# Decode attention with a gated dense branch: part of one weight load split into sixteen transfers of a few rows

## The chip, the cores and the metric

One core of a Trainium2 chip. The metric is the device time of one execution in microseconds (us).

## What is computed

A decode step for two sequences of one token each (B = 2), model width 448, everything in float32:

```
g = sigmoid((x * gate_w).sum(-1))
q = (x @ wq)                       # 16 heads of 256
p = softmax(q . k_cache / 16)      # 4096 cached positions per head
a = concat(p . v_cache) @ wo
b = relu(x @ w1 + b1)**2 @ w2 + b2
out = g * a + (1 - g) * b
```

The caches hold 2 x 16 x 4096 x 256 numbers each, 134 MB; with the weights some 290 MB pass through the core, each byte once.

## The kernel before

The work of attention is cut into 16 rounds: 8 pairs of heads times 2 sequences. A round takes 8.4 MB of keys and 8.4 MB of values. 128 partitions hold them, 64 for each head of the pair, and each partition has 64 positions in one contiguous row of 64 KB. Keys go into two buffers in turn (`keys[0]`, `keys[1]`; both are named `k` in the profile), values into one (`vals`, named `v`). In a round VectorE multiplies the keys by the query in place (L218) and sums over the 256 (L235), TensorE brings the maxima together, ScalarE takes the exponential (L255), and TensorE multiplies the probabilities by the values (`values`, in a loop of 15 rounds on the chip, and once more for the last). The output of each head pair is normed, turned and kept in `oT`.

The buffers carry weights as well. Before the rounds `keys[1]` holds `wq` (7.3 MB), and the lower part of `vals`, up to `spare` = 12,544 numbers of each partition, holds `wf`, that is `w1` and `w2` laid out by rows (6.4 MB; 50,176 B of each partition). After the last round's values have been used, `vals` takes `wo` in five pieces.

All large loads go through one queue, that of SyncE (SP), by the helper `load` (its issue is L116). The order is: `wq` (L170), the keys of round 0 (L171), `wf` (L172), the keys of round 1 (L206, held until TensorE has finished with `wq`), the values of round 0 (L232, held until TensorE has finished with `wf` and the dense branch), and from there keys (L248) and values (L243) in turn, each held until its buffer is free. The first three wait for nothing. `pk` (x, gate, b1; L169) and `b2` (L173) are issued by ScalarE (ACT).

Each load raises a semaphore by 16 when it has landed; `load` returns the count so far. For `wf` that is `FL`. TensorE waits for it at one place, ahead of the hidden layer (the matmuls into `fin`), where the code before has `pe.wait_ge(FL.h, 16)`. Behind that wait TensorE computes the hidden layer and turns it (`sm`), VectorE applies bias, relu and square (L228 to L231), and TensorE adds the second dense product into `acc`. All matmuls go through the helper at L289.

At the end TensorE takes the last values (`po`), turns them (`ot`), and multiplies `oT` with `wo`: 24 blocks into `acc`, 8 into `fin`; the first 16 blocks need the first piece of `wo`. Then VectorE copies the result (L276), and SP sends it out (L279).

Of the kernel before, what the change touches and what calls it, by code (L numbers as in the profile page):

```python
# [10 lines left out]
P = 128  # L11
# [2 lines left out]
WO_CUTS = (0, 16, 24, 28, 31, 32)  # L14
V_CUT = 48
HELP = 24


class Count:
# [16 lines left out]
def gated_mix_kernel(nc, b2, wq, wf, wo, k_cache, v_cache, out):  # L36
# [18 lines left out]
    pe, dve, act, pool, sp = nc.tensor, nc.vector, nc.scalar, nc.gpsimd, nc.sync  # L55
# [3 lines left out]
    def sb(name, *free):  # L59
        return nc.alloc_sbuf_tensor(name, [P, *free], F32)[:]  # L60
# [5 lines left out]
    vals = sb("v", PLACE)  # L66
# [30 lines left out]
    QL, FL, BL, SL = (Count(nc, n + "_landed") for n in ("wq", "wf", "b2", "small"))  # L97
# [9 lines left out]
    spare = w2_at + FC * D  # L107
# [3 lines left out]
    def kv(cache, r):  # L111
        t, b = rounds[r]
        return cache[b, 2 * t:2 * t + 2].rearrange("h (p j) d -> (h p) (j d)", j=KEYS)

    def load(dst, src, sem, after=None):
        ins = sp.dma_start(dst, src)  # L116
        if after:
            after[0].on(ins, after[1])
        return sem.up(ins, 16)
# [49 lines left out]
    SL.up(act.dma_start(pk, wq[:, 3 * N + N // 2:3 * N + N // 2 + PK]), 16)  # L169
    load(keys[1][:, :3 * N + N // 2], wq[:, :3 * N + N // 2], QL)  # L170
    load(keys[0], kv(k_cache, 0), KL[0])  # L171
    load(vals[:, :spare], wf, FL)  # L172
    BL.up(act.dma_start(b2r, b2), 16)  # L173


# [31 lines left out]
    for r, (t, b) in enumerate(rounds):  # L207
# [4 lines left out]
        elif r == 4:  # L212
            dve.wait_ge(AC.h, AC_QB[-1])
        help = HELP if r == R - 1 else 0
        s = scores[r == R - 1]

        def times_q(lo, hi):
            return DV.up(KL[r % 2].on(dve.tensor_tensor(kt[:, lo:hi], kt[:, lo:hi], q.unsqueeze(1).to_broadcast([P, hi - lo, DH]), op=ALU.mult), 16 * (r // 2 + 1)))  # L218
# [7 lines left out]
        n = times_q(help, KEYS)  # L226
# [139 lines left out]
            pe.wait_ge(AC.h, AC_QB[i - 4])  # L366
        done(mm(QBANK[i % 4], halves[:, u * B + b, :], qs[:, a, :]), TE_QB[i])

    pe.wait_ge(FL.h, 16)
    for c in range(CF + 1):  # L370
        for n in range(4):
            if c < CF:
# [36 lines left out]
    for i, (t, k) in enumerate(blocks):  # L409
# [9 lines left out]
        n = i - early  # L419
# [72 lines left out]
```

## Time and profile before

| | us |
|---|---|
| median of 3 runs | 676.64 |
| lowest and highest run | 676.58, 892.45 |
| profiled execution, its own time | 676.61 |
| its span, first to last instruction | 675.3 |
| VectorE busy | 560.0 |
| TensorE busy (matmuls) | 218.2 |
| ScalarE busy | 45.8 |

SP's queue is q1 in the profile, ACT's is q10, and q8 and q14 carry instructions to the engines. A packet is one contiguous piece that one of the core's 16 DMA engines moves. The queue view lists packets, MB and the time of the packets as a share of 16 engines over the window that was asked for; a packet counts in the window where it starts, with its whole time, so in a window of a few hundred ns the share can pass 100%. "Under 512 B" counts the small packets; in SP's queue of this kernel these are, but for the output, the 4-byte writes that raise a semaphore when an engine has done its part of a transfer. In the timeline a row has start, duration, engine, line, operation, tiles, and in brackets how long the engine was idle before and what ended that. "SPq" rows are SP's issues.

### The profile page before, as it was taken

The numbers are of one execution on the slowest core, as the hardware profiler recorded it, in microseconds if no ns is written. First come the engines' busy times: TensorE is split into PE (matmuls) and PEld (weight loads), VectorE is DVE, ScalarE is ACT, GpSimd is POOL, SyncE is SP. The second block draws the span as 40 slices with busy tenths as digits, with TensorE's granted clock in tenths as the row PEclk, the third lists the DMA queues.
The fourth block names the chain that finished last, engine by engine and source line by source line (L and its number), as shares of the span: only waits on it lengthen the run. The fifth ranks groups of instructions, "written<-read, shape, count | busy, mean of one in ns | idle before, by whom it ended". The sixth has DMA issues, their size and how long they took to land. (4 is left out here: it accounts for less than half of the span.)

```text
span 675.3 us, 3522 instructions
## 1 busy us (share of the span) xinstructions
PE 218.2 (32%) x1522; PEld 67.9 (10%) x1522; DVE 560.0 (83%) x120; ACT 45.8 (7%) x159; POOL 2.1 (0%) x15
## 2 busy tenths in 40 slices
PE   0725042140605124060503206060411506050386
PEld 0111001010101101010100101010110101010022
DVE  1067999999979797998979798997979799797920
ACT  0121000000000000000000000000000000001400
POOL 1000000000000000000000000000000000000000
PEclk9977556585756557575655757575665757576577
DMA  9999999999999999999999999999999999999997
GB/s 381 431 453 421 435 435 436 435 435 431 431 435 435 435 435 435 435 435 435 435 435 435 435 435 435 435 431 435 435 427 435 435 435 435 435 435 431 422 415 305
DMA packets 5923, 289.63 MB, mean 429 GB/s; under 512 B 797, under 2 KB 926, under 8 KB 1182
## 3 DMA queue, kind: packets, MB, share of 16 engines
q1 hardware_dynamic: 5772, 289.54, 99.2%
q8 instruction: 3, 0.05, 0.0%
q10 hardware_dynamic: 146, 0.02, 0.0%
q14 instruction: 2, 0.02, 0.0%
HBM read 289.55 MB, written 0.00 MB: 429 GB/s over the span
## 5 line engine op out<-in xcount | busy, mean ns | idle before, releaser
L218 DVE TENSOR_TENSOR k<-k,q 128x16384 f32<-128x16384 f32 (+2 forms) x17 | 275.7, 16220 | 52.4 <-DMA k<-in_k_cache_dram 52.4
L235 DVE TENSOR_REDUCE s<-k 128x64 f32<-128x16384 f32 x15 | 258.2, 17211 | 0.0
L289 PE MATMUL po<-v,p 128*4 128x512 f32 x960 | 139.6, 746 | 294.4 <-PEq L293 294.4
L289 PEld LDWEIGHTS po<-v,p 128*4 128x4 f32 x960 | 26.8, 99 | 394.4 <-issue 394.4
L194 ACT ACTIVATE o<-po 128x512 f32<-128x512 f32 x16 | 9.6, 597 | 438.0 <-PE po L289 438.0
L289 PE MATMUL mt<-ident,m 128*64 128x64 f32 x64 | 7.6, 328 | 82.3 <-PEq L293 82.3
L289 PE MATMUL ot<-rl,o 128*128 128x2 f32 x128 | 16.4, 250 | 15.6 <-PEq L293 15.6
L289 PEld LDWEIGHTS ot<-rl,o 128*128 128x128 f32 x128 | 15.5, 191 | 30.0 <-issue 30.0
L255 ACT ACTIVATE p<-s,nb 64x64 f32<-64x64 f32 x30 | 10.5, 350 | 96.1 <-DVE nb L239 95.9
L289 PE MATMUL sm<-rsm,ones 128*128 128x2 f32 x32 | 8.9, 348 | 21.3 <-PEq L293 21.3
L239 DVE TENSOR_REDUCE nb<-mt 128x1 f32<-128x64 f32 x16 | 3.6, 225 | 13.0 <-PE mt L289 13.0
L176 DVE TENSOR_TENSOR y<-pk 128x8 f32<-128x8 f32 x1 | 0.2, 169 | 16.8 <-DMA pk<-in_wq_dram 16.8
L289 PEld LDWEIGHTS mt<-ident,m 128*64 128x64 f32 x64 | 5.1, 200 | 83.9 <-issue 83.9
L235 DVE TENSOR_REDUCE s_last<-k 128x40 f32<-128x10240 f32 x1 | 10.8, 10810 | 0.0
L289 PEld LDWEIGHTS sm<-rsm,ones 128*128 128x128 f32 x32 | 8.0, 310 | 23.7 <-issue 23.7
L273 DVE COPY wide<-oT 128x2 f32<-128x2 f32 x8 | 0.7, 165 | 11.7 <-ACT oT L195 11.7
L224 ACT ACTIVATE k<-k 128x256 f32<-128x256 f32 x24 | 9.6, 400 | 8.5 <-DVE k L218 8.5
L289 PE MATMUL fin<-v,pk 128*2 128x448 f32 x32 | 4.9, 775 | 16.0 <-DMA v<-in_wf_dram 16.0
L289 PE MATMUL pq<-k,pk 128*2 128x512 f32 x64 | 9.9, 787 | 0.0
L289 PE MATMUL po<-k,p 128*4 128x512 f32 x64 | 9.4, 753 | 0.5 <-DMA k<-in_v_cache_dram 0.5
L276 DVE COPY y<-fin 128x112 f32<-128x112 f32 x1 | 0.3, 275 | 10.2 <-PE fin L289 10.2
L289 PE MATMUL acc<-v,oT 128*2 128x448 f32 x48 | 7.1, 765 | 2.1 <-DMA v<-in_wo_dram 2.1
(64 smaller groups left out, 68.3 us busy)
## 6 DMA issues: line engine op xcount, KB each, us to landing
k<-in_wq_dram SPq DMA_DIRECT2D x1, 7168.0 KB, 19.7
v<-in_wf_dram SPq DMA_DIRECT2D x1, 6272.0 KB, 53.0
k<-in_v_cache_dram SPq DMA_DIRECT2D x1, 6144.0 KB, 37.8
v<-in_wo_dram SPq DMA_DIRECT2D x1, 3584.0 KB, 17.9
k<-in_v_cache_dram SPq DMA_DIRECT2D x1, 2048.0 KB, 42.4
v<-in_wo_dram SPq DMA_DIRECT2D x1, 1792.0 KB, 21.8
v<-in_wo_dram SPq DMA_DIRECT2D x1, 896.0 KB, 23.6
v<-in_wo_dram SPq DMA_DIRECT2D x1, 672.0 KB, 24.7
```

Source lines behind the costliest of these rows:

```text
L176: DV_Y = DV.up(SL.on(dve.tensor_tensor(y, xT[:, :CF + 1, :].rearrange("p c b -> p b c"), pk[:, 10:14].unsqueeze(1).to_broadcast([P, B, CF ...
L194: OC.up(TE.on(act.activation(o, po, AF.Copy), te_val(r)))
L218: return DV.up(KL[r % 2].on(dve.tensor_tensor(kt[:, lo:hi], kt[:, lo:hi], q.unsqueeze(1).to_broadcast([P, hi - lo, DH]), op=ALU.mult), 16 ...
L224: ins = act.activation(kt[:, j], kt[:, j], AF.Copy, accum_out=s[:, j:j + 1])
L235: DV_S = DV.up(DV.on(dve.tensor_reduce(s[:, help:], kt[:, help:], axis=AX.X, op=ALU.add), n))
L239: DV_NB = DV.up(TE.on(dve.tensor_reduce(nb, mt[:, :64], axis=AX.X, op=ALU.max, negate=True), te_mt(r)))
L255: e = act.activation(p8[z, :, hh:hh + 3:2], s[z].rearrange("p (m s) -> p m s", s=2), AF.Exp, bias=nb[z], accum_out=rsm[z, hh:hh + 1])
L273: DV_W = dve.tensor_copy(wide[:, n, 0:W:16], o_block(t, k))
L276: DV_Y4 = DV.up(TE.on(dve.tensor_copy(y4, fin[:, :DQ]), TE_FIN))
L289: return pe.matmul(dst, lt, rhs, start=start, stop=stop)
```

## The change

The first 128 numbers (512 B) of each of the 128 rows of `wf` leave the one transfer, which now takes 49,664 B of each row. They follow it in sixteen transfers on the same queue, of 8, 1, 15, 14, 13 and so on down to 2 rows; the rows are taken in order from partition 0 to 127. All raise the same semaphore, and TensorE waits for the sum of the seventeen.

```diff
+FIRST = 128
+ROWS = [8, 1] + list(range(15, 1, -1))
...
     load(keys[0], kv(k_cache, 0), KL[0])
-    load(vals[:, :spare], wf, FL)
+    load(vals[:, FIRST:spare], wf[:, FIRST:], FL)
+    p0 = 0
+    for n in ROWS:
+        load(vals[p0:p0 + n, :FIRST], wf[p0:p0 + n, :FIRST], FL)
+        p0 += n
+    assert p0 == P
     BL.up(act.dma_start(b2r, b2), 16)
...
-    pe.wait_ge(FL.h, 16)
+    pe.wait_ge(FL.h, FL.n)
     for c in range(CF + 1):
```

SP's instructions from the program's start, before (a size is partitions x numbers; `pe`, `dve` are the semaphores of TensorE and VectorE):

```order
L116 DMA k<-in_wq_dram 128x14336 [waits barrier_Pool_Activation_PE_DVE_SP_release]
L116 DMA k<-in_k_cache_dram 128x16384
L116 DMA v<-in_wf_dram 128x12544
L116 DMA k<-in_k_cache_dram 128x16384 [waits pe]
L116 DMA v<-in_v_cache_dram 128x16384 [waits pe]
```

And with the change, the same place down to the fourth of the small transfers (lines have moved by two):

```order
L118 DMA k<-in_wq_dram 128x14336 [waits barrier_Pool_Activation_PE_DVE_SP_release]
L118 DMA k<-in_k_cache_dram 128x16384
L118 DMA v<-in_wf_dram 128x12416
L118 DMA v<-in_wf_dram 8x128
L118 DMA v<-in_wf_dram 1x128
L118 DMA v<-in_wf_dram 15x128
L118 DMA v<-in_wf_dram 14x128
```

The small ones go on in this way; here their last three, and what follows on SP:

```order
L118 DMA v<-in_wf_dram 4x128
L118 DMA v<-in_wf_dram 3x128
L118 DMA v<-in_wf_dram 2x128
L118 DMA k<-in_k_cache_dram 128x16384 [waits pe]
L118 DMA v<-in_v_cache_dram 128x16384 [waits pe]
```

The sixteen stand between `wf` and the keys of round 1, without a wait of their own; SP has 57 issues where it had 41. On the other engines no instruction moves.

## The prediction

> **What bounds the kernel now.** I read the page's slices first, then the chain that ended last, then VectorE and the SP queue in order of time, and last narrow windows of the DMA view.
>
> ```profile
> DMA  9999999999999999999999999999999999999997
> GB/s 381 431 453 421 435 435 436 435 435 431 431 435 435 435 435 435 435 435 435 435 435 435 435 435 435 435 431 435 435 427 435 435 435 435 435 435 431 422 415 305
> q1 hardware_dynamic: 5772, 289.54, 99.2%
> ```
>
> The 16 DMA engines are busy 99.2% of the span in SP's queue (q1), at 435 GB/s in most of the 40 slices (16.9 us each). VectorE has the next largest share, but from the fifth round on it waits for keys; the first two such waits, and the last but one:
>
> ```profile
> 152.38 17.23 DVE L218 TENSOR_TENSOR k<-k,q 128x16384 f32<-128x16384 f32 x1 [0.42 <-DMA k<-in_k_cache_dram]
> 191.09 17.22 DVE L218 TENSOR_TENSOR k<-k,q 128x16384 f32<-128x16384 f32 x1 [2.87 <-DMA k<-in_k_cache_dram]
> ...
> 578.09 17.23 DVE L218 TENSOR_TENSOR k<-k,q 128x16384 f32<-128x16384 f32 x1 [2.86 <-DMA k<-in_k_cache_dram]
> ```
>
> From 191.09 to 578.09 lie ten rounds, so 38.70 us a round, 2.87 of them VectorE's idle time. For this stretch the DMA view says:
>
> ```profile
> DMA packets 2882, 167.79 MB, mean 434 GB/s; under 512 B 320, under 2 KB 320, under 8 KB 320
> q1 hardware_dynamic: 2880, 167.77, 100.2%
> ```
>
> 2,560 packets of 64 KB and 320 tiny ones, 16 for each of 20 transfers: one completion marker per engine and transfer. The engines have no gap, markers or not, and one engine moves 434/16 = 27.1 bytes a ns. The end of the chain:
>
> ```profile
> 646.14 17.91 DMA v<-in_wo_dram
> 664.05 0.14 issue
> 664.18 7.15 PE acc L289 x48
> 671.33 1.89 PE fin L289 x72
> ```
>
> ```profile
> 664.18 1.68 PE L289 MATMUL acc<-v,oT 128*2 128x448 f32 x8 [2.06 <-DMA v<-in_wo_dram]
> ```
>
> TensorE stands idle for 2.06 us until the first piece of `wo` has landed. So the end is set by the moment at which the slowest DMA engine finishes that piece; an earlier landing would be worth time, a later one costs its whole delay. How uneven the engines are is seen by counting markers in narrow windows. At the landing of `wf` (53.35:53.87, then 54.2:54.25), and of the piece of `wo` (661.75:662.3, 662.6:662.78, 663.5:663.7):
>
> ```profile
> DMA packets 30, 0.98 MB, mean 1891 GB/s; under 512 B 15, under 2 KB 15, under 8 KB 15
> DMA packets 2, 0.07 MB, mean 1311 GB/s; under 512 B 1, under 2 KB 1, under 8 KB 1
> ```
>
> ```profile
> DMA packets 22, 0.16 MB, mean 287 GB/s; under 512 B 11, under 2 KB 11, under 8 KB 11
> DMA packets 11, 0.11 MB, mean 637 GB/s; under 512 B 3, under 2 KB 3, under 8 KB 3
> DMA packets 8, 0.09 MB, mean 430 GB/s; under 512 B 2, under 2 KB 2, under 8 KB 2
> ```
>
> At `wf`, 15 engines finish within 0.5 us and one some 0.35 later. At `wo` eleven finish by 662.3, three near 662.7, and two only past 663.5, at least 1.2 us behind the eleven. I take the two for those that carried the instruction fetches of 16 KB at 58.3 and 104.3 (windows 58.3:59.3 and 104.3:104.5):
>
> ```profile
> q8 instruction: 1, 0.02, 6.5%
> q8 instruction: 1, 0.02, 32.0%
> ```
>
> 6.5% of 16 x 1.0 us and 32.0% of 16 x 0.2 us are 1.04 and 1.02 us of one engine each. Nothing evens that out later, since every engine gets the same bytes of each transfer. Which engine is which the trace does not say.
>
> **The change, priced.** It moves no byte more: 128 rows x 512 B leave the one transfer of `wf` and come in sixteen small ones behind it, on the same queue.
>
> Removed: each engine has 8 of the 128 rows, so 8 x 512 B at 27.1 bytes a ns, 0.151 us per engine.
>
> Added: no transfer of so few rows of 512 B is in the trace. How many packets a transfer of few rows makes is seen on the ACT queue and at the output:
>
> ```profile
> q10 hardware_dynamic: 146, 0.02, 0.0%
> ```
>
> ```profile
> DMA packets 12, 0.00 MB, mean 6 GB/s; under 512 B 12, under 2 KB 12, under 8 KB 12
> ```
>
> 146 are 128 rows of `pk` with 16 markers, and one row of `b2` with one. The output (window 674.7:675.3) has 4 outer rows of two pieces: 8 packets and 4 markers. So a transfer of n rows, n up to 15, should take n engines, with one packet and one marker on each. That makes 128 packets and 128 markers over all engines. One marker, alone in a window of 7 ns (53.385:53.392); 15 packets of 112 B (4.3:4.9); 21 of 1,792 B with 3 markers (671.75:672.35):
>
> ```profile
> q1 hardware_dynamic: 1, 0.00, 8.0%
> ```
>
> ```profile
> q10 hardware_dynamic: 15, 0.00, 2.0%
> ```
>
> ```profile
> q1 hardware_dynamic: 24, 0.04, 16.5%
> ```
>
> Times 16 engines and the window: a marker 9 ns; 112 B 0.192/15 = 13 ns; 1,792 B (1.584 - 0.027)/21 = 74 ns. On the line between, 512 B are 13 + 400 x 61/1680 = 28 ns, an estimate. A small row costs its engine 37 ns. An engine that gets c of the 128 changes by 37c - 151 ns. The bounds are c = 0 and c = 16 (one row of each transfer): -0.15 and +0.44 us. Spread evenly, c = 8, it is +0.15. What counts is the larger change of the two late engines, which is above the mean if the shares differ: I take **+0.2 us** and keep both ends.
>
> The Trainium skill, in "DMA: Bandwidth & Descriptors", section "Why a DMA increments its semaphore by 16 and not by 1", says that such a transfer runs on as many engines as divide its row count, up to 16, and always on the lowest-numbered. By that the shares are 16, 15 ... 9, 7 ... 0 from engine 0 to 15, a stair, and the mean over all pairs of the larger change is +0.26, so 676.9 where an even spread gives 676.8; the ends stay as above, and no row here shows which engines are taken.
>
> On the queues: SP issues sixteen transfers more. Their price, and the room for it:
>
> ```profile
> 1.65 0.43 SPq L116 DMA_DIRECT2D v<-in_wf_dram  x1
> 31.64 0.33 SPq L116 DMA_DIRECT2D k<-in_k_cache_dram  x1
> 66.40 0.33 SPq L116 DMA_DIRECT2D v<-in_v_cache_dram  x1
> ...
> 646.14 2.23 SPq L116 DMA_DIRECT2D v<-in_wo_dram  x5
> ```
>
> Five in a row take 2.23 us, so sixteen take 7.1 and are out by 9.3, while SP has nothing to issue until 31.64. Nothing else of SP's stands behind them. Cost 0; even an SP held up until 53 would still feed the ring in time, since only then does `wf` run out. Past that each us would be lost in full. No other queue is passed: the two loads on ACT's queue wait for nothing and stand apart.
>
> The wait on `wf` now holds TensorE until all seventeen transfers have landed, up to 0.44 us later. Behind it stand the hidden layer and the first values load; VectorE waits for the former:
>
> ```profile
> 54.67 4.91 PE L289 MATMUL fin<-v,pk 128*2 128x448 f32 x32 [16.04 <-DMA v<-in_wf_dram]
> 61.35 0.19 DVE L228 TENSOR_TENSOR hb<-sm,pk 128x28 f32<-128x28 f32 x1 [4.33 <-PE sm L289]
> ```
>
> VectorE passes that delay into its first rounds, where it bounds itself; it meets the DMA stream at 152.38 with 0.42 us to wait and idles 2.87 a round from then on, so what it brings along is covered by the stream's own shift and by that idle time (without it: up to 0.44). The values load goes out at 66.40 and is due when the second keys' first engine is through. Its markers (window 72.68:73.2):
>
> ```profile
> DMA packets 28, 0.92 MB, mean 1765 GB/s; under 512 B 14, under 2 KB 14, under 8 KB 14
> ```
>
> Fourteen engines end there, so 6.3 us are spare. The sum: 676.61 us, the profiled execution's own time (span 675.3), + 0.2 = 676.8. The median before is 676.64, 0.03 above that execution, which alters nothing.
>
> **Rivals.**
>
> First, a small transfer costs its engine more than its packets, as the ring changes from one to the next. For it: no row shows sixteen so short ones in line. Against it: the 320 markers above stand in a stream with no gap. With 0.1 us each, engine 0's sixteen add 1.6 if it is late already: 676.6 + 0.44 + 1.6 = 678.6; with a share of eight, 676.6 + 0.15 + 0.8 = 677.6.
>
> Second, the end on the other side: the next small transfer starts on an engine only when the one before is complete. The place is SP's ring at the end of `wf`. The nearest price is from an issue to its first packets:
>
> ```profile
> 673.54 0.68 SPq L279 DMA_DIRECT2D out_dram<-y  x1
> ```
>
> Its 12 packets all lie past 674.7, so some 1.2 us; sixteen on one engine are 19 us, 696 in all. It would decide from 13.5/16 = 0.85 us each. The same gapless stretch speaks against it: 20 transfers of one round trip each would have cost 24 of its 387 us. The Trainium skill, in the same page's section "Rules for kernel authors", holds that transfers under 64 KB are mostly overhead, and its section "Anatomy of one DMA" puts 2.0 us on each; paid sixteen times in line that would be an estimate of 32 us and 709. Its rule for a single transfer need not hold for a queue of them, and the rows above bear out the queue.
>
> Third, the instruction fetches fall otherwise. SP's program is longer by sixteen; a further 1.0 us fetch on one of the two late engines gives 677.8; with the two on engines that finish early, the group near 662.7 would decide, some 0.9 us sooner, 675.9. Against: the two fetches that matter lie at 58 and 105, where SP does nothing new.
>
> Fourth, the engines read memory out of step and the stream gets faster. For it: some slices stand under 435. Against: the even ones do not. With slices 9 to 39 all at 435 the sum of the shortfalls, 57/435 x 16.9, gives 2.2 us: 674.4.
>
> **Numbers.** Forecast 0.78 (676.4 to 677.1, time 676.8), first rival 0.10, second 0.02, third 0.06, fourth 0.03, 0.01 for what no row shows. The range, 676.3 to 678.0, holds the forecast, half of the first rival and half of the third. A measurement of this kernel tells about 2%, 13.5 us, from no change: faster beyond that 0.01 (the unknown), slower 0.02 (the second rival), within it 0.97.
>
> **What would show it.** SP's queue gains 256 packets (5,772 to about 6,028) and the bytes stay. Small transfers are out by 9.3 us, TensorE starts on `wf` between 54.5 and 55.1, the rounds stay at 38.70 us, and the wait before the first block of `wo` moves from 2.06 by tenths, as late markers there move by 37c - 151 ns. If the small transfers show gaps between their packets, or the landing of `wf` slips by over a us, the price of a row is wrong; if the round changes from 38.70, engine timing matters to the memory and my sum lacks it; if the two late engines are no longer two, the fetches moved.

## The result, and the profile after

The changed kernel takes 678.69 us (median of 7 runs, 678.21 to 680.22) against 676.75 before, taken beside it: 1.0031 times as long, 95% interval 1.0019 to 1.0043. (One run of before, 892.45 us, is left out of the ratio as disturbed; the medians alone give 1.0029.) The profiled execution took 678.42 us with a span of 677.1, 1.81 us more than that of before. The forecast was 676.8, in a range of 676.3 to 678.0: the loss is some ten times as large as forecast, though still far under 2%.

The DMA section of the page after:

```profile
DMA packets 6179, 289.63 MB, mean 428 GB/s; under 512 B 925, under 2 KB 1182, under 8 KB 1438
q1 hardware_dynamic: 6028, 289.54, 99.2%
```

The queue has 6,028 packets, 256 more, as the count of packets and markers said. The bytes are the same. VectorE in order of time, at its first wait for keys since round 0, and near the end of the even part:

```profile
192.91 17.23 DVE L225 TENSOR_TENSOR k<-k,q 128x16384 f32<-128x16384 f32 x1 [1.78 <-DMA k<-in_k_cache_dram]
...
579.93 17.23 DVE L225 TENSOR_TENSOR k<-k,q 128x16384 f32<-128x16384 f32 x1 [2.86 <-DMA k<-in_k_cache_dram]
...
618.63 17.30 DVE L225 TENSOR_TENSOR k<-k,q 128x6144 f32<-128x6144 f32 x2 [2.87 <-DMA k<-in_k_cache_dram]
```

The round is 38.70 us as before (579.93 to 618.63), so the stream's speed has not changed. Before, the first of these rows stood at 191.09 and the second at 578.09: VectorE is 1.82 us late at the first and 1.84 at the second, so the time was lost before the even part. SP in order of time:

```profile
1.64 6.79 SPq L118 DMA_DIRECT2D v<-in_wf_dram  x17
30.26 0.36 SPq L118 DMA_DIRECT2D k<-in_k_cache_dram  x1
73.17 0.35 SPq L118 DMA_DIRECT2D v<-in_v_cache_dram  x1
```

The small transfers are out by 8.4 us, somewhat before the forecast 9.3. But the first values load goes out at 73.17, 6.8 us later than before (66.40). TensorE and VectorE show why:

```profile
57.29 5.72 PE L296 MATMUL fin<-v,pk 128*2 128x448 f32 x32 [20.04 <-DMA v<-in_wf_dram]
65.77 1.60 PE L296 MATMUL acc<-b2r,gP 1*2 1x448 f32 x2 [1.04 <-DVE hT L238]
67.30 5.83 PE L296 MATMUL acc<-v,hT 128*2 128x448 f32 x28
```

TensorE's wait on `wf` ends at 57.29 instead of 54.67. Then both products take longer, at a lower granted clock (column PEclk, third from the right; first the changed kernel's second dense product, then that of before):

```profile
65.80:73.10 7.30, 7.30 (x30) 1.03 (x30) 7.30 (x1) 0.00 (x0) 0.00 (x0) 0.53 0.97 422
```

```profile
62.40:66.30 3.90, 3.90 (x30) 0.73 (x29) 3.90 (x1) 0.00 (x0) 0.00 (x0) 1.00 1.24 538
```

The same 30 matmuls ran at full clock before and at 0.53 now. So the load is 2.62 us late from the wait, 0.81 from the hidden layer, and 3.35 from the second product. Only the first of the three is the change's own work. Of the sixteen profiled kernels of this document, the second product took 7.1 to 7.4 us in ten, `keys_stair` and `keys_even` below among them, which load `wf` whole; 5.7 us in four; and 4.0 us in two, of which the kernel before is one.

Two things are seen in the DMA view after. First, the stretch in which the small transfers are recorded (53.3:54.24):

```profile
DMA packets 288, 1.11 MB, mean 1186 GB/s; under 512 B 144, under 2 KB 272, under 8 KB 272
q1 hardware_dynamic: 288, 1.11, 370.5%
```

They are 144 markers (16 of them of the large part of `wf`), 128 rows and the first 64 KB packet of each of the 16 engines. 370.5% of 16 x 0.94 us are 55.7 us; less 128 x 27 ns and 144 x 9 ns, 51.0 remain for the sixteen large packets, 3.19 us each where 2.42 is usual. The small packets have about their forecast length in the records (27 ns), and the packet behind them pays 0.76 us more on average. The sixteen are not alike: in the packet records eight took 2.48 to 2.82 us and eight 3.51 to 4.30. Second, at the end of the keys of round 1 (72.96:73.6):

```profile
DMA packets 8, 0.07 MB, mean 102 GB/s; under 512 B 7, under 2 KB 7, under 8 KB 7
```

Seven engines write their marker for the keys, and one large packet starts. Before, each marker had a large packet right behind it; here early engines have nothing to do, since the values load was issued only at 73.17. By the packet records the seven stood for 1.2 us on average.

Where the slowest engine stands, by markers: at the keys, the first values, the second keys and the first piece of `wo` (windows 75.36:75.4, 93.94:94.72, 115.0:115.06 and 665.0:665.5):

```profile
DMA packets 2, 0.07 MB, mean 1638 GB/s; under 512 B 1, under 2 KB 1, under 8 KB 1
DMA packets 32, 1.05 MB, mean 1344 GB/s; under 512 B 16, under 2 KB 16, under 8 KB 16
DMA packets 2, 0.07 MB, mean 1092 GB/s; under 512 B 1, under 2 KB 1, under 8 KB 1
DMA packets 16, 0.20 MB, mean 401 GB/s; under 512 B 2, under 2 KB 2, under 8 KB 2
```

The slowest marker of the keys is at 75.38 (74.51 before), 0.87 us late. At the first values it is 94.70 against 93.86, 0.84 late, and all sixteen lie within 0.8 us, where before they spanned 1.8: the early engines have lost their lead. At the second keys it is 115.04 against 113.21, 1.83 late, and one engine alone is there. Between the two lies the instruction fetch at 103.96 (window 103.9:104.0):

```profile
q8 instruction: 1, 0.02, 60.1%
```

It takes 0.96 us of one engine. Before, an engine ahead of the slowest could give up a part of that time without setting the end; now that lead is gone. From there the delay stays: at the first piece of `wo` the last marker is at 665.44, 1.82 us later than before (663.62), and TensorE starts on `wo` at 666.03, 1.85 us later. Behind that the end has changed. TensorE in order of time, and a stretch of the chain that ended last:

```profile
666.03 6.39 PE L296 MATMUL acc<-v,oT 128*2 128x448 f32 x48 [2.77 <-DMA v<-in_wo_dram]
...
674.01 0.96 PE L296 MATMUL fin<-v,wide 128*17 128x112 f32 x32 [0.44 <-DMA v<-in_wo_dram]
```

```profile
648.79 25.18 DMA v<-in_wo_dram
673.97 0.04 issue
674.01 1.00 PE fin L296 x32
```

The 48 products with `wo` took 6.39 us where they took 7.15 before, and then TensorE stood idle for 0.44 us until the last piece of `wo` had landed. So the end still hangs on the stream, but on its last piece and no longer on the first.

### The profile page after: what moved, and what is told of

Its sections match the earlier page's. It is cut to its first block, busy times and chain, and to the rows that moved or that the text cites. A ratio compares the mean times of both kernels' runs of the same rounds, so it can differ in the third digit from the quotient of the medians.

```text
span 677.1 us, 3538 instructions
## 1 busy us (share of the span) xinstructions
PE 221.4 (33%) x1522; PEld 68.3 (10%) x1522; DVE 559.9 (83%) x120; ACT 45.8 (7%) x159; POOL 2.1 (0%) x15
## 3 DMA queue, kind: packets, MB, share of 16 engines
q1 hardware_dynamic: 6028, 289.54, 99.2%
## 5 line engine op out<-in xcount | busy, mean ns | idle before, releaser
L296 PE MATMUL po<-v,p 128*4 128x512 f32 x960 | 141.2, 753 | 287.5 <-PEq L300 287.5
```

What stands on the lines that cost most here:

```text
L296: return pe.matmul(dst, lt, rhs, start=start, stop=stop)
```

## The experiments

After the result there were two theories. **A**: each small transfer holds its engine by some 0.1 us beyond its packets. **B**: `wf` is complete late, so the first values load is late, and early engines run dry at 73 us. The rivals were A alone, B alone, and the 512 B pieces as such. Each kernel was timed beside the one before the change, whose medians were 676.69 to 676.82. Mean marker times are means of the sixteen markers of one load, from the packet records.

**One piece instead of sixteen.**

```diff
     load(vals[:, FIRST:spare], wf[:, FIRST:], FL)
-    p0 = 0
-    for n in ROWS:
-        load(vals[p0:p0 + n, :FIRST], wf[p0:p0 + n, :FIRST], FL)
-        p0 += n
+    load(vals[:, :FIRST], wf[:, :FIRST], FL)
```

> The 512 B columns are still loaded apart, but in one transfer of 128 rows instead of sixteen. Theory A (each small transfer holds its engine by about 0.2 us until its marker is written; the count of transfers per engine is what costs): 676.8 us, within 0.3 of the kernel before, TensorE starts on wf near 54.8, the first values load goes out near 66.5. Rival (the 512 B packets themselves, or the cut rows, cost): 678 to 679 us, since all 128 packets of 512 B stay.

676.95 us against 676.82, ratio 1.0004 (0.9995 to 1.0013). The stretch 53.33:54.19 of its DMA view:

```profile
DMA packets 174, 1.05 MB, mean 1219 GB/s; under 512 B 31, under 2 KB 159, under 8 KB 159
q1 hardware_dynamic: 174, 1.05, 290.7%
```

The same 128 rows, with 31 markers: 290.7% of 16 x 0.86 us, less the small ones, leaves 2.42 us for each of 15 large packets. So rows of 512 B in one transfer cost nothing that shows here: the medians differ by 0.13 us, and the interval leaves room for 0.9. The count of transfers costs. A detail of the expectation missed: the values load went out at 69.84 and not 66.5, with TensorE at 0.55 of its clock in the second product. The engines still did not run dry.

**The small ones ahead of the rest of `wf`.**

```diff
-    load(vals[:, FIRST:spare], wf[:, FIRST:], FL)
     p0 = 0
...
+    load(vals[:, FIRST:spare], wf[:, FIRST:], FL)
```

> The same sixteen small transfers, issued ahead of the rest of wf instead of behind it, so that TensorE's wait on wf ends near 55 to 56 instead of 57.3 and the first values load goes out well before the keys' first engine is through at 73. Theory A+B (the small transfers delay the slowest engine by 0.85 us, the dry ring at 73 costs the other 0.95): 677.5 us. Rival A alone: 678.5. Rival B alone (only the dry ring costs): 676.7.

678.08 us against 676.82, ratio 1.0019 (1.0009 to 1.0028). The values load went out at 71.41, and by the packet records one of the first engines stood for some 0.4 us, so part of B may have come back with the later landing; the time lies between the first two expectations. It does not separate the theories; the next kernel does.

**The small ones behind `wf`, with a wait of their own.**

```diff
-    load(vals[:, FIRST:spare], wf[:, FIRST:], FL)
+    cut = spare - FIRST
+    load(vals[:, :cut], wf[:, :cut], FL)
     p0 = 0
     for n in ROWS:
-        load(vals[p0:p0 + n, :FIRST], wf[p0:p0 + n, :FIRST], FL)
+        load(vals[p0:p0 + n, cut:spare], wf[p0:p0 + n, cut:], TL)
...
+    pe.wait_ge(TL.h, TL.n)
     for c in range(FC):
         ins = add(hT[:, c, :], vals[:, w2_at + c * D:w2_at + (c + 1) * D])
```

> The sixteen small transfers stand behind wf as in the changed kernel, but carry the last 128 numbers of each row, which belong to w2, with a semaphore of their own that TensorE waits on only ahead of the second dense product. The hidden layer starts near 54.6 as before the change, the values load goes out near 66.5, and no engine runs dry at 73. Theory A+B: 677.5 us, with the keys of round 1 landing last near 75.4. Rival A alone: 678.5. Rival B alone: 676.7.

677.79 us against 676.82, ratio 1.0016 (1.0007 to 1.0026). The keys' slowest marker was at 75.22, and the values load went out at 70.27 (not near 66.5 as expected, with the second product at 7.4 us). At 73 there was no gap (72.98:73.3):

```profile
DMA packets 8, 0.26 MB, mean 819 GB/s; under 512 B 4, under 2 KB 4, under 8 KB 4
```

Four markers, four large packets behind them. A remains, about 1.0 us: TensorE starts on `wo` at 665.15, 0.97 us later than before, where in the changed kernel it is 1.85. About half of the changed kernel's loss is gone with the dry ring. The two intervals overlap between 1.0019 and 1.0026; of the eleven runs here three are longer than the shortest of the changed kernel's seven (678.21).

**A late values load without small transfers.** The kernel before, with the hidden layer done twice:

```diff
-    for c in range(CF + 1):
-        for n in range(4):
+    for again in range(2):
+        for c in range(CF + 1):
+            for n in range(4):
...
```

> The kernel before the change, with TensorE doing the hidden layer's 16 products twice (same result), so that the first values load goes out 5 to 9 us later, at 71.5 to 75 us, while the keys' first engine is through at 72.7. No small transfers. Theory A+B: a dry ring by itself costs 0.3 to 1.5 us, so 677 to 678 us, and the values' markers come closer together. Rival A alone (the slowest engine never idles, so a dry ring of the early ones costs nothing): 676.7.

678.46 us against 676.82, ratio 1.0024 (1.0014 to 1.0034), with runs from 676.76 to 679.30; the median lies above the expected 677 to 678. The load went out at 71.73; the markers of the first values lie within 92.97 to 94.30 where before they spanned 92.03 to 93.86. So B costs by itself. Not all of it is the stream: in its profiled execution (678.21) TensorE started on `wo` at 664.98, 0.80 us later than before, and the other 0.8 us lie behind that. The 48 products with `wo` took 7.44 us where they took 7.15 before, and the last products stood idle 0.30 us for the last piece of `wo`, a wait that the kernel before does not have. The stretch 664:670 has the granted clock at 0.50 there, and 0.57 before:

```profile
664.00:670.00 6.00, 5.02 (x28) 1.03 (x32) 0.11 (x2) 0.00 (x0) 0.00 (x0) 0.50 0.98 409
```

**Small transfers where nothing waits.** `wf` whole, and the keys of round 1 cut instead: their last 128 numbers of each row in the same sixteen transfers (first), in eight of 16 rows (second), and 768 numbers in sixteen (third). VectorE waits for them only before it takes those keys.

```diff
-    load(keys[1], kv(k_cache, 1), KL[1], (TE, TE_Q1))
+    at = PLACE - LAST
+    load(keys[1][:, :at], kv(k_cache, 1)[:, :at], KL[1], (TE, TE_Q1))
+    p0 = 0
+    for n in ROWS:
+        load(keys[1][p0:p0 + n, at:], kv(k_cache, 1)[p0:p0 + n, at:], TL)
+        p0 += n
...
+        if r == 1:
+            dve.wait_ge(TL.h, TL.n)
```

> wf is loaded in one piece as before the change; the same sixteen transfers of 512 B rows stand behind the keys of round 1 (the last 128 numbers of each row, with a semaphore of their own, which VectorE has no need of before 80). The values load goes out as early as before, so no ring runs dry. Theory A: each small transfer costs its engine 0.12 us, 8 on average, less 0.15 us of bytes taken away: the mean marker of the first values comes 0.8 us later than before, and the time is 677.4 to 678.1 us. Rival (the sixteen matter only by delaying TensorE's work on wf): 676.8.

678.10 us against 676.80, ratio 1.0018 (1.0009 to 1.0027); the mean marker of the first values 0.87 us later. A, with TensorE's work on `wf` out of it. Its stretch 72.59:74.57:

```profile
q1 hardware_dynamic: 288, 1.11, 176.2%
```

By the sum used above, 3.19 us for a large packet, as in the changed kernel.

> As keys_stair, but eight transfers of 16 rows: every one of the 16 engines gets the same eight small transfers. Theory A: all engines 8 x 0.12 - 0.15 = 0.8 us later, 677.6 us, with the spread of the markers as before. Rival (what costs is the unevenness, or a transfer on fewer than 16 engines): 676.9.

677.53 us, ratio 1.0010 (1.0001 to 1.0019); mean marker 0.63 later. The stretch 72.69:74.67:

```profile
q1 hardware_dynamic: 288, 1.11, 161.9%
```

2.91 us for a large packet, 0.49 more than usual on eight small transfers per engine, so 0.06 us each where the stair has 0.095 (0.76 / 8). Even shares cost about three quarters of the stair's delay. That fits a price for each transfer on each engine that it uses, lower where it uses all 16; that the price grows evenly with the count is not shown.

This kernel also shows the price for the semaphore by itself. One engine is a full us behind the other fifteen, and the trace's record of the semaphore has its last seven steps at 75.27, 75.44, 75.60, 75.76, 75.93, 76.08 and 76.24, that is some 0.16 us apart, while the small packets of that engine are all recorded by 74.67.

> As keys_stair, with rows of 3,072 B, whose packet takes some 0.12 us itself. If a small transfer costs a fixed 0.085 us beside its packet: the mean marker of the first values comes 0.8 us later than before, the spread of the engines grows to 5 us or so, and the time is 678 to 679.5 us. If 0.12 us is a least time per transfer, which a packet of 0.12 us fills: the mean marker comes 0.1 us later, and only the unevenness counts (engines from 0.9 us earlier to 1.1 later), 676.3 to 677.9 us.

679.01 us, ratio 1.0031 (1.0019 to 1.0043). The time lies in the range of the larger expectation, but not by its mechanism: the mean marker came 1.69 us later, twice what it gave, and the spread of the first values' markers was 2.2 us (93.10 to 95.30) and not 5. Neither form of the price holds for rows of 3 KB. By the packet records, packets of 121 ns were stretched to over 300, and the first 64 KB packets of engines with few small rows, begun by 72.5, took 4.0 us.

**Where the rows go.** As keys_stair, with partitions 64 to 127 in one transfer and 0 to 63 in eight transfers of 8 rows, four partitions apart or consecutive (the comments are added here):

```diff
+ROWS = [slice(a, a + 32, 4) for h in (0, 32) for a in range(h, h + 4)]   # own
+ROWS = [slice(a, a + 8) for a in range(0, 64, 8)]                        # crossed
...
+    for rs in [slice(64, 128)] + ROWS:
+        load(keys[1][rs, at:], kv(k_cache, 1)[rs, at:], TL)
```

> As keys_stair, but of the last 128 numbers of the keys' rows partitions 64 to 127 come in one transfer, and 0 to 63 in eight transfers of 8 rows that lie four partitions apart (a, a+4 ... a+28). Theory P (a small row is slow because it goes to partitions that another engine is filling at that moment, and both stand; rows four apart go to the partitions that the same engine fills in a load of 128 rows): the first 64 KB packets behind the small ones take nearly their usual 2.42 us on the eight engines, and the mean marker of the first values comes 0.1 to 0.3 us later than before, less than in crossed_512 by 0.2 or more. Theory F (each small transfer costs a fixed 0.08 to 0.12 us beside its packet, wherever it goes): the same as crossed_512, 0.3 to 0.6 us.

> As own_512, with the eight transfers of 8 rows taking consecutive partitions (0 to 7, 8 to 15 ...), as the changed kernel's rows do. Theory P: the first 64 KB packets behind are stretched on all or most engines, the mean marker of the first values 0.4 to 0.8 us later than before. Theory F: as own_512, 0.3 to 0.6 us, stretched on eight engines alone.

677.57 us, ratio 1.0012 (1.0003 to 1.0021), and 677.30, ratio 1.0010 (1.0001 to 1.0019), against 676.72; mean markers 0.53 and 0.46 later. The stretches 72.61:74.55 and 72.6:74.66:

```profile
q1 hardware_dynamic: 240, 1.11, 161.1%
```

```profile
q1 hardware_dynamic: 240, 1.11, 150.3%
```

With 96 markers and 128 rows each that is 2.86 and 2.83 us for a large packet: no difference. In the records of own_512 nine of the sixteen packets took over 2.9 us, the others at most 2.61; in crossed_512 eight did, the others at most 2.51. Theory P falls for rows of 512 B, and F fits: some 0.1 us per small transfer (0.43 x 16 / 64), on about as many engines as carry them.

> As own_512 with rows of 3,072 B. Theory P: the packets of 3,072 B run at their 121 ns and the mean marker of the first values comes 0.1 to 0.4 us later than before; 1 us or so less than in crossed_3k. Theory F: the same as crossed_3k.

> As crossed_512 with rows of 3,072 B. Theory P: packets of 3,072 B take up to 300 ns and more, the mean marker of the first values comes 0.8 to 1.8 us later than before (1.7 with sixteen transfers in the stair). Theory F: the same as own_3k, 0.3 to 0.6 us.

677.88 us, ratio 1.0017 (1.0008 to 1.0026), and 678.53, ratio 1.0029 (1.0017 to 1.0041); mean markers 1.08 and 1.14 later. The loads land alike, so P fails here too, but F's 0.3 to 0.6 us does not hold either. What makes rows of 3 KB dearer stays open.

**Both together.** stair_tail, with products of the hidden layer done once more and thrown away, so that the values load is late again: 8, then 20, then 32 of them. (The loop below gives 20 and 32; for 8 it took two chunks once. The comment in it is added here.)

```diff
+    for i in range(5):          # 8 for the third
+        c = i % 3
+        for n in range(4):
+            mm(fin[32 * n:32 * n + B, :D], xT[:, c, :], vals[:, c * F + n * D:c * F + (n + 1) * D])
```

> stair_tail, with half of the hidden layer's products done twice (same result), so that the first values load goes out some 2.5 us later, near 73, as it does in the changed kernel. Theory A+B: the dry ring comes back on top of the small transfers, and the time is that of the changed kernel, 678.4 to 679.2 us. Rival (with the small transfers there, the late engines never idle and the dry ring costs nothing more): 677.8 us as stair_tail.

677.83 us against 676.69, ratio 1.0018 (1.0009 to 1.0027): it tells nothing of B, since the load went out at 69.64, with TensorE at a higher clock in the second product, and no engine ran dry.

> stair_tail, with 20 products of the hidden layer done once more than needed (thrown away), so that the first values load goes out at 71.5 to 75 us. The keys' first engine is through at 73.0. Theory A+B: 678.2 to 679.5 us, and the values' markers come closer together than the keys'. Rival (the late engines never idle, so the dry ring costs nothing on top): 677.8 us as stair_tail.

678.81 us against 676.78, ratio 1.0031 (1.0019 to 1.0043), the changed kernel's ratio. The load went out at 71.23. At 72.9:73.5, at the first values (93.1:94.7), and at the second keys (112.4:114.05, 115.2:115.3):

```profile
DMA packets 8, 0.07 MB, mean 109 GB/s; under 512 B 7, under 2 KB 7, under 8 KB 7
DMA packets 32, 1.05 MB, mean 655 GB/s; under 512 B 16, under 2 KB 16, under 8 KB 16
DMA packets 31, 1.05 MB, mean 636 GB/s; under 512 B 15, under 2 KB 15, under 8 KB 15
DMA packets 5, 0.26 MB, mean 2621 GB/s; under 512 B 1, under 2 KB 1, under 8 KB 1
```

Seven engines done and one large packet; then sixteen markers within 1.6 us; then, behind the fetch at 99.36, one engine alone, 1.3 us behind the other fifteen. By the packet records the seven got their first large packets of the values between 73.32 and 74.68, that is 2.1 to 3.5 us after the issue. This is the changed kernel's pattern, made without a late `wf`. B adds to A.

> The same with 32 such products: the load goes out some 2 us later, at 73.5 to 78 us. Theory A+B: 679 to 682 us, by as much more than tail_and_late5 as the load is later, once all engines wait for it. Rival: 677.8 us while the load is out before 75, and only past that more.

680.53 us, ratio 1.0060 (1.0047 to 1.0074), clear of `stair_tail` and its 1.0016. The load went out at 75.13; the first values' markers lie between 95.9 and 96.4, and all engines had waited. B grows with the delay, as expected.

## Why the prediction was wrong

**What bounds the kernel** held in the main: the stream and, at its end, the slowest engine's part of the first piece of `wo`; the rounds stayed at 38.70 us, and the delay of that landing, 1.82 us by the slowest marker, came out at the end as 1.81. That the two agree so closely is luck. In the changed kernel the products behind that landing were 0.76 us shorter, and the end then waited for the last piece of `wo`, a wait that the prediction did not have.

**The price of a small row failed, in size.** The step was "A small row costs its engine 37 ns". The packets and markers do take 27 and 9 ns, but they are not the whole price. In the stream each small transfer costs an engine 0.06 to 0.11 us more on average, which are seen in the next large packet. In the semaphore it costs more than that: the last marker of `wf` is recorded by 54.24 and TensorE goes on only at 57.29, where before 0.45 us lay between. With the 0.16 us from step to step that `keys_even` shows, an engine with a row in each of the sixteen transfers is late by some 2.6 us, and 2.62 is what the wait lost. The first rival had this mechanism and, with 0.1 us, the right size for the stream. That its 678.6 us is near the measured time is luck, since it puts all of the loss on one engine's sixteen transfers and has no dry ring. It held a chance of 0.10 because 320 markers with no gap in the even part were read as proof that a change of transfers is free. There every marker follows eight packets of 64 KB, some 19 us, which leave time for whatever the marker needs; this reason is argued. A price that shows only when transfers follow one another within tens of ns was not on the trace. The Trainium skill ("DMA: Bandwidth & Descriptors", section "Queues, rings and completion order") says that a marker is written only once all earlier writes of its engine have landed; that fits what is seen, but no run here separates the marker from the rest of a transfer. Its 2.0 us per transfer (section "Anatomy of one DMA"), which that section gives for transfers that GpSimd issues and not SP, were not paid one after another: here a small transfer cost about a twentieth of that in the stream, and 0.16 us in the semaphore.

**The cover of the values load failed.** The step was "so 6.3 us are spare", and with it "up to 0.44 us later". The wait became 2.6 us longer, as a consequence of the first error. The spare time was one execution's: with the second product at half clock, as in one_piece with its load at 69.84, it is 3 us. The full clock in the profiled execution before was luck, since only two of the sixteen profiled kernels had it. And the load needs a margin: out at 71.23 (tail_and_late5), engines done at 72.95 found nothing yet, while out at 70.27 (stair_tail), engines done at 73.00 found their packets. So some 2 us of the 6.3 were never there. The dry ring therefore took both, the late wait and the low clock: with the second product as long as before, the load would have gone out near 69.8 (an estimate, 73.17 less 3.35), ahead of the 70.27 that was early enough. Each kernel has one trace, so how often the changed kernel's ring runs dry is not known. This is the half that no rival named: the prediction followed the wait to VectorE, whose idle time does cover it, and set the other branch off against a number.

**Queues** held: the seventeen issues of `wf` took 6.8 us in a time when SP had nothing to do, and nothing was held up.

**The fetches** stand as the reason why one or two engines are late, but the step by which only their own change counts was too simple. In the changed kernel the dry ring took the lead from the early engines, and the next fetch then set how far the last engine was behind. Which engine a fetch meets was not varied; that it decides is argued from the markers of two kernels.

**The other rivals**: the one on the far side, 1.2 us per transfer, is out by a factor of ten; a faster stream did not appear.

By medians the loss of 1.94 us divides into 1.0 to 1.3 for A (stair_tail 0.97, keys_stair 1.30) and the rest, 0.6 to 1.0, for B.

## What to carry to other kernels

Where DMA engines never idle, as here, the price of more transfers is not seen in how small packets are recorded but in the packet behind them and in when the semaphore is complete; one transfer of 128 rows of 512 B cost nothing that shows, sixteen of a few rows cost a microsecond. When a change can delay the landing that frees a buffer, follow it to the next load's issue and compare that with the moment at which the first engine runs out, less some 2 to 3 us (1.7 were too few here, 2.7 enough), and take TensorE's products at the lowest granted clock that the traces show. A dry moment of the early engines is not free either: it takes the lead that hides later hold-ups.

## What was not expected of the hardware

The recorded length of a small packet (27 ns for 512 B) tells nothing of the 0.1 us that its transfer costs in the stream, or of the 0.16 us between two steps of its semaphore. The second dense product, the same 30 matmuls, took between 3.9 us at a granted clock of 1.00 and 7.3 us at 0.53, and that moved the issue of a load by over 3 us. Rows of 3,072 B in small transfers delayed the mean engine by 1.1 to 1.7 us, more than rows of 512 B (0.5 to 0.9), and stretched packets on engines that carried few of them; no run explains that.
